# A recurrent attention kernel with a relu-squared MLP: instructions put out in a written order, loads in halves, smaller state transposes

## The chip, the cores and the metric

The kernel runs on one core of a Trainium2 chip. The metric is the time of one execution on the device, in microseconds (us). Each number below is from the hardware profile of one execution, or from repeated timed executions, as the text says.

## The reference

Two stages follow one another. The first walks over 768 positions and keeps a 40 x 40 state for each of 4 batch entries and 8 heads; its output, laid out as 3072 tokens of 320 values, goes through a two-layer MLP with relu squared between the layers.

```python
B, H, S, D = 4, 8, 768, 40
state = np.zeros((B, H, D, D))
for t in range(S):
    y[:, :, t] = np.einsum('bhd,bhde->bhe', r[:, :, t], state)
    Sa = np.einsum('bhde,bhe->bhd', state, a[:, :, t])
    state = state * w[:, :, t][:, :, None, :] - np.einsum('bhd,bhe->bhde', Sa, b[:, :, t]) \
        + np.einsum('bhd,bhe->bhde', v[:, :, t], k[:, :, t])
x = y.transpose(0, 2, 1, 3).reshape(3072, 320)
out = np.maximum(x @ w_in, 0.0) ** 2 @ w_out      # 320 -> 2048 -> 320
```

## The kernel before

**Steps.** The recurrence is computed in blocks of 64 positions, for two batch entries at a time. That gives 12 blocks x 2 pairs = 24 steps, numbered g = 0 to 23; step g continues the state of step g - 2. Each step is a graph of small operations with names. An operation X of step g is called X.g in this text.

**Loads.** LW, LK and LB (line L423) bring w, k and b of the step from device memory through SP's queue, each as two transfers, one for each batch entry. Tiles: Wf, KBf. LA brings a (tile Af), through SP for steps 0 to 3 and through POOL from step 4 on. LV0 and LV1 (L499) bring v, LR (L433) brings r, both through POOL. POOL also brings the MLP weights, wi, wj (tile WIN) and wo (tile WOUT), once. Step 0's LK and LB go through ACT. The buffers of w, k, b and a hold four steps.

**Decay.** LN (ACT, L438) takes the logarithm of w, LO (POOL) its low part, and the matmuls CS and CE (TensorE, the tiles cs and ce) sum it over positions. EXN and EXE (ACT) take exponentials. KBS0 and KBS1 (POOL, L487) scale k and b into KB, AS scales a into A, GLM makes the state's decay.

**Attention.** KB is transposed into KBT: for steps 0 to 5 by TensorE (KT) and a copy, from step 6 on by a DMA transpose that SP issues (KX, L519). AT and RT transpose a and r. EB multiplies KBT with them (L561); EBE masks the product on DVE (L565). XV, X0 and COR form the corrected values x (L576, L584, L598), with ACT copies UA and UB between and MA and MB after (L589, L603). ST (L613, L618) forms the new state, STE (DVE) scales and writes it as STB, SX (L632) transposes it, and SXE (DVE) copies it out as SB. VT (L643), CP, CPE, YC (L657), YS and YE make the output y, and XT and XTE transpose it.

**MLP.** For two halves of the hidden columns: U0 or U1 (L697), then UX and UY (L706) write hp; RL (ACT, L711) applies relu, SQ (DVE, L715) squares it, and D0 to D3 (L724) accumulate fo. OE (ACT) and OST (SP, L735) write the result.

**TensorE's three forms.** Each matmul operation has a mode: M uses the array whole, R splits its rows and C its columns.

**The order.** The kernel is written in one program order; each engine, and each DMA queue, then takes its own instructions strictly in that order, and semaphores make an engine wait for the others. The order comes from the class Plan: it simulates the engines and queues when the kernel is built, with a duration for each operation (the argument dur of add) and costs for each transfer (the argument dma: a number of units and the time of one). Of the operations that an engine could start earliest it takes the one with the lowest place, from the tables PLACE and SHIFT, and adds STAY to the place of one that changes TensorE's mode. Buffers in PSUM come from four rings: S (3 buffers), D, HP and F (one each). Where this simulation leaves TensorE idle ahead of D0.0, the end of the function puts warm-up matmuls (tile warm, L823), of 512 columns each.

Of the kernel before, what the change touches and what calls it, by code (L numbers as in the profile page):

```python
# [32 lines left out]

SHIFT = {}
SHIFT[0] = {
    "zK1": 2018.27, "VT": 2349.81, "AT": 1866.43, "UY0": -3353.72, "KX": -2197.21, "zL0": 1908.62, "zV0": 1900.43,
    "wj2": 1808, "wj1": -1942.98, "EB": 1944.74, "KT": -2891.79, "zF0": 2034.22, "UB": 1935.23, "CS": -2785.17,
    "MA": 2049.64, "U0": 2170.04, "wp0": 2098.6, "KBS0": 1881.72, "RT": 1943.66, "zA1": 2269.37, "RTE": 820.24,
    "EBE": 2195.88, "wo0": 2050.8, "zF2": 2322.28, "SELB": 2324.1, "U1": 1925.05, "TI": 1848.81, "zK2": -2247.96,
    "wi1": -2297.07, "ID": -3595.09, "LV1": 2335.3, "zS1": 2314.64, "ATE": 2366.64, "zL1": 2233.74, "UI": 2813.84,  # L40
    "XT": 2190.97, "zR1": -1897.12, "CE": 2105.63, "LN": -3231.66, "OST": -1905.28, "MB": -1865.15, "X0": 1784.49,
    "CPE": 1714.17, "LV0": 1164.1, "ones": 1737.78, "SEL": 2278.83, "CP": 2605, "UA": -2188.66, "D1": 1958.77,
# [130 lines left out]
class Plan:  # L173
# [3 lines left out]
    DMA_LAG = 2.0  # L177
# [5 lines left out]
    def add(self, name, g, eng, dur, fn, deps=(), mode=None, alloc=None, frees=None, dma=None):  # L183
        o = Op()
# [670 lines left out]
```

## Time and profile before

| quantity | value |
|---|---|
| median of 8 runs | 271.67 us (269.47 to 276.55) |
| the profiled execution: its time | 271.3 us |
| the profiled execution: its span | 269.6 us |
| busy: PE, DVE, ACT, POOL | 246.5, 177.3, 164.2, 164.2 us |
| DMA: moved | 33.75 MB in 111,913 packets |

The span is the part of the execution that the profile covers; 1.7 us of the time lie around it. A busy PE is a bad measure here, since the ends of pipelined matmuls are modelled: the distances from start to start, in the timeline, are of more use. In the views, a line with an engine's name and q (SPq, POOLq) tells of the queue's issuing; PEld is TensorE's weight load.

### The profile page before, as it was taken

How to read it: one execution, taken by the hardware profiler on the slowest of the kernel's cores; microseconds unless marked ns; L12 is line 12 of the kernel's file. 1: busy time of each engine (PE TensorE's matmuls, PEld its weight loads, DVE VectorE, ACT ScalarE, POOL GpSimd, SP SyncE). 2: the span in 40 equal slices, each digit the busy share in tenths (PEclk: the TensorE clock that was granted, in tenths of full speed). 3: DMA queues.
4: the chain of work that ended last, by engine and by line, in shares of the span. 5: the costliest groups of instructions: out<-in, count | busy, mean ns of one | idle time of the engine just before them, and what ended most of it. 6: DMA issues, size and time to landing. Idle time of an engine off the chain costs nothing.

```text
span 269.6 us, 13153 instructions
## 1 busy us (share of the span) xinstructions
PE 246.5 (91%) x5817; PEld 197.6 (73%) x5817; DVE 177.3 (66%) x296; ACT 164.2 (61%) x289; POOL 164.2 (61%) x244
## 2 busy tenths in 40 slices
PE   6869968999989998999999989899999999999980
PEld 2447756697778886878888867788887888888750
DVE  7827756685847865856866856766875866786520
ACT  2355644877657756756866756766775686365440
POOL 2869766994875777576778757678767591400000
PEclk9986999999999999999999999999999999999998
DMA  6999999977999979978979987986989362210010
GB/s 111 155 183 169 189 203 150 154 139 142 124 164 122 162 132 145 150 150 140 165 140 143 120 149 119 156 157 133 127 159 106 83 128 46 62 29 27 12 38 26
DMA packets 111913, 33.75 MB, mean 125 GB/s; under 512 B 101232, under 2 KB 109808, under 8 KB 111856
## 3 DMA queue, kind: packets, MB, share of 16 engines
q1 hardware_dynamic: 100272, 20.79, 51.6%
q0 software_dynamic: 9472, 11.80, 24.3%
q8 instruction: 45, 0.74, 1.2%
q10 hardware_dynamic: 2112, 0.33, 0.7%
q14 instruction: 12, 0.10, 0.1%
HBM read 28.84 MB, written 3.93 MB: 122 GB/s over the span
## 4 chain that ended last, share of the span: by engine, by line
PE 51%; DMA 21%; SPq 15%; ACT 3%; issue 3%; POOL 2%; DVE 2%; POOLq 0%; ACTq 0%; DVEq 0%
SPq L423 15%; PE fo L724 12%; PE hp L706 12%; DMA KBT<-KB 10%; DMA Wf<-in_w_dram 7%; PE hp L697 3%; DMA KBf<-in_b_dram 3%; PE vt L643 2%; PE sx L632 2%; PE rt L532 2%; PE cp L561 2%; ACT RL L711 2%; PE eb L561 2%; PE y L657 2%; DMA KBf<-in_k_dram 1%
## 5 line engine op out<-in xcount | busy, mean ns | idle before, releaser
L487 POOL TENSOR_TENSOR KB<-KBf,EXN 128x320 bf16<-128x320 f32 x45 | 45.4, 1024 | 44.2 <-PE y L657 39.2
L711 ACT ACTIVATE RL<-hp 128x1024 bf16<-128x1024 f32 x46 | 47.1, 1024 | 37.7 <-PE hp L706 37.6
L724 PE MATMUL fo<-WOUT,GT 128*128 128x320 bf16 x384 | 63.1, 299 | 1.1 <-DVE GT L715 1.1
L706 PE MATMUL hp<-XT,WIN 128*128 128x128 bf16 x736 | 52.4, 220 | 0.0
L565 DVE TENSOR_TENSOR EBM<-eb,MASK 128x1024 bf16<-128x1024 f32 x24 | 29.3, 1222 | 29.3 <-PE eb L561 29.2
L706 PEld LDWEIGHTS <-WIN 128*128 128x128 bf16 x768 | 44.1, 98 | 3.9 <-issue 0.3
L715 DVE TENSOR_TENSOR GT<-RL 128x1024 bf16<-128x1024 bf16 x48 | 38.2, 795 | 10.4 <-ACT RL L711 10.4
L724 PEld LDWEIGHTS <-GT 128*128 128x128 bf16 x384 | 33.4, 97 | 12.4 <-DVE GT L715 2.2
L499 POOL DMA_DIRECT2D Vf<-in_v_dram x48 | 33.7, 705 | 0.3 <-issue 0.3
L438 ACT ACTIVATE LNW<-Wf 128x320 f32<-128x320 f32 x24 | 11.2, 468 | 31.5 <-DMA Wf<-in_w_dram 16.2
L565 DVE TENSOR_TENSOR CPM<-cp,MASK 128x1024 bf16<-128x1024 f32 x24 | 29.2, 1216 | 1.4 <-PE cp L561 1.4
L624 DVE TENSOR_TENSOR STB<-st,GLM 128x640 bf16<-128x640 f32 x22 | 18.1, 824 | 15.7 <-PE st L618 13.1
L423 POOL DMA_DIRECT2D Af<-in_a_dram x40 | 27.4, 691 | 0.0
L446 POOL TENSOR_TENSOR LLO<-LNW 128x320 bf16<-128x320 f32 x24 | 17.5, 728 | 9.3 <-ACT LNW L438 9.3
L589 ACT ACTIVATE UZ<-x 64x320 bf16<-64x320 f32 x48 | 20.7, 432 | 3.9 <-PE x L576 2.5
L603 ACT ACTIVATE VM<-x 64x320 bf16<-64x320 f32 x48 | 20.6, 430 | 3.3 <-PE x L598 2.6
L493 POOL TENSOR_TENSOR A<-Af,EXE 128x320 bf16<-128x320 f32 x24 | 20.8, 868 | 1.6 <-DMA Af<-in_a_dram 0.7
L647 DVE COPY VMT<-vt 128x1024 bf16<-128x1024 bf16 x24 | 16.6, 691 | 3.8 <-PE vt L643 2.3
L697 PE MATMUL hp<-XT,WIN 64*128 64x128 bf16 x368 | 18.2, 218 | 0.8 <-ACT RL L711 0.8
L460 ACT ACTIVATE EXN<-cs 128x640 f32<-128x640 f32 x24 | 16.8, 699 | 2.0 <-PE cs L454 1.9
L503 ACT ACTIVATE VM<-Vf 128x640 bf16<-128x640 f32 x24 | 17.6, 733 | 0.5 <-DMA Vf<-in_v_dram 0.2
L729 ACT ACTIVATE OSB<-fo 128x320 f32<-128x320 f32 x24 | 10.4, 434 | 10.1 <-PE fo L724 9.8
(90 smaller groups left out, 459.4 us busy)
## 6 DMA issues: line engine op xcount, KB each, us to landing
Wf<-in_w_dram SPq DMA_DIRECT2D x48, 80.0 KB, 6.0
Vf<-in_v_dram POOLq DMA_DIRECT2D x48, 80.0 KB, 5.4
out_dram<-OSB SPq DMA_DIRECT2D x24, 160.0 KB
KBf<-in_b_dram SPq DMA_DIRECT2D x46, 80.0 KB, 3.2
KBf<-in_k_dram SPq DMA_DIRECT2D x46, 80.0 KB, 6.0
Af<-in_a_dram POOLq DMA_DIRECT2D x40, 80.0 KB, 4.5
RB<-in_r_dram POOLq DMA_DIRECT2D x24, 80.0 KB, 4.4
WOUT<-in_moe_w_out_dram POOLq DMA_DIRECT2D x2, 640.0 KB, 10.7
```

The lines of the kernel that those rows point to most:

```text
L423: q_.dma_start(out=V(dst, step * be, [(40, 8), (1, 40)], 64 * h, 64), in_=tok(src, b0 + be))
L487: (nc.vector if g < 3 and be else nc.gpsimd).tensor_tensor(out=V(kb, 512 * be, [(64, 8), (1, 40)]), in0=V(kbf, 320 * be, [(40, 8), (1, 40) ...
L493: nc.gpsimd.tensor_tensor(out=V(at, 0, [(64, 8), (1, 40)]), in0=V(af, 0, [(40, 8), (1, 40)]), in1=V(exe, 0, [(40, 8), (1, 40)]), op=ALU.mult)
L499: nc.gpsimd.dma_start(out=V(vf, 320 * be, [(40, 8), (1, 40)], 64 - 64 * be, 64), in_=tok(v, b0 + be))
L565: nc.vector.tensor_tensor(out=V(dst, 0, [(64, 16), (1, 64)]), in0=V(psum(key, g), 0, [(64, 16), (1, 64)]), in1=V(MASK, 0, [(0, 16), (1, 64 ...
L589: nc.scalar.activation(out=V(uz, 320 * be, [(1, 320)], 64 * be, 64), in_=V(psum("x", g), 0, [(1, 320)], 64 * be, 64), func=ACTF.Copy, scal ...
L603: nc.scalar.activation(out=V(vm, 512 * be, [(64, 8), (1, 40)], 64 * be, 64), in_=V(psum("x", g), 0, [(40, 8), (1, 40)], 64 * be, 64), func ...
L697: mm(out=V(p, 512 * s + 128 * i, [(1, 128)]), lhsT=wcol(1 + s, blk, 64 * s, 64), rhs=xt[64 * s:64 * s + 64, 128 + 128 * s:256 + 128 * s], ...
L706: mm(out=V(p, 512 * s + 128 * i, [(1, 128)]), lhsT=wcol(x, blk, 0, 128), rhs=xt[:, 128 * x:128 * x + 128], start=False, stop=i == 3 and x > 0)
L711: nc.scalar.activation(out=rl[:], in_=psum(hk, g)[:], func=ACTF.Relu)
L715: nc.vector.tensor_tensor(out=gt[:], in0=rl[:], in1=rl[:], op=ALU.mult)
L724: mm(out=p[:, 0:320], lhsT=gt[:, 512 * s + 128 * i:512 * s + 128 * i + 128], rhs=WOUT[:, DM * blk:DM * blk + DM], start=blk == 0, stop=blk ...
```

## The change

The tables and the choosing simulation are taken out. The program order is now written down as a list, ORDER, of all operations; an entry ~n stands for n warm-up matmuls. Plan only walks through that list, checks that each operation's dependencies have been put out, and hands out the PSUM buffers. The orders of all engines and queues differ from before. The two halves of each load LW, LK, LB and LA become operations of their own, with an a or b at the end of the name, which can stand apart; a half of LK or LB depends only on the KBS of its own half four steps earlier. The names in ORDER show this. The state transposes SX take 104 of STB's 128 rows, since rows 104 to 127 hold no state values, so each of the 8 transposes has a moving operand of 104 columns. The other changed lines alter only numbers that nothing reads any more (the third argument after the engine and dma).

```diff
-PERIOD = 23.56
-PLACE = {
-    "zK1": -384.93, "VT": -379.85, "AT": -379.8, "UY0": -379.8, "KX": -379.8, "zL0": -378.59, "zV0": -366.03,
...
-SWITCH = 0.095
-STAY = 48.55
-WINDOW = {"PE": 0, "ACT": 0, "DVE": 0, "POOL": 0, "SP": 0}
+ORDER = """
+TBL.0 zK1.0 LWa.0 ones.0 UI.0 LWb.0 ID.0 UE.0 LKa.0 LAb.0 MASK.0 zL0.0 SELB.0 LBa.0 LWb.2 zS1.0 zV0.0 LBb.0 zR3.0
+LAa.0 zU1.0 zK0.0 LKb.0 zA0.0 LWa.2 TI.0 LN.0 zR0.0 zR1.0 zR2.0 zF0.0 LO.0 LWb.1 zF2.0 LV1.0 ~8 CS.0 LWa.1 TE.0
+EXN.0 LV0.0 zS0.0 ~1 CE.0 zU0.0 LKb.1 LR.0 zA1.0 zS2.0 EXE.0 KBS0.0 zF1.0 LAb.1 LAa.2 KBS1.0 AS.0 zV1.0 ~6 KT.0
+LAb.2 zL1.0 LN.1 AT.0 wi1.0 ATE.0 LN.2 LR.1 LKa.1 KTE.0 VC.0 LO.2 LAa.1 zV2.0 ~5 EB.0 LO.1 EBE.0 CE.2 LBa.1 wi2.0
+CE.1 SEL.0 LV0.1 EXE.1 XV.0 zF3.0 UB.0 GLM.0 LBb.1 LV1.1 zV3.0 UA.0 zK2.0 ~3 COR.0 LWa.3 wp0.0 LR.2 CS.1 MA.0 wj2.0
+RT.0 MB.0 LWb.3 EXN.1 AS.1 ~1 VT.0 LKb.2 RTE.0 VTE.0 KBS0.1 LWa.4 EXE.2 ~2 AT.1 I2.0 KBS1.1 RT.1 wj1.0 ST.0 ATE.1
+CP.0 GLM.2 KT.1 AS.2 CPE.0 LBb.2 LKa.2 LN.3 LV0.2 KTE.1 VC.1 ~3 CS.2 LBa.2 LV1.2 STE.0 EXN.2 YC.0 LAb.3 wj0.0 RTE.1
+YE.0 EB.1 LO.3 SX.0 LAa.3 EBE.1 LR.3 CE.3 LKa.3 EXE.3 SXE.0 LBa.3 XV.1 KBS0.2 KBS1.2 CS.3 UB.1 AT.2 UA.1 wi0.0 KT.2
+ATE.2 EXN.3 COR.1 LV1.3 KTE.2 RT.2 MA.1 LKb.3 wp1.0 XT.0 MB.1 EB.2 XTE.0 VC.2 LBb.3 AS.3 VT.1 EBE.2 RTE.2 U1.0 LWb.4
+GLM.1 UX1.0 wo0.0 UY1.0 VTE.1 LV0.3 AT.3 RL1.0 LWa.5 ST.1 ATE.3 XV.2 KBS0.3 X0.2 STE.1 LWb.5 CP.1 UB.2 U0.0 KBS1.3
+LBb.4 UY0.0 UA.2 CPE.1 UX0.0 wo1.0 KT.3 RL0.0 LBa.4 SX.1 KTE.3 COR.2 LN.4 SXE.1 YC.1 MA.2 EB.3 LO.4 YE.1 RT.3 MB.2
+XT.1 LAb.4 RTE.3 CE.4 XTE.1 LKa.4 LR.4 SQ0.0 VT.2 EXE.4 LAa.4 ST.2 LKb.4 EBE.3 D0.0 LV0.4 D1.0 VC.3 LWa.6 LV1.4
...
+XTE.3 LWb.9 KBS0.6 EB.5 U0.3 EBE.5 LWb.10 CE.6 LV0.7 VT.4 LBb.8 EXE.6 UY0.3 LV1.7 VC.5 VTE.4 LKb.9 D2.2 AS.6 LN.8
+ST.4 XV.5 LAa.7 STE.4 X0.5 KX.6 CP.4 UB.5 LO.8 UX0.3 CPE.4 UA.5 D3.2 RL0.3 LAa.8 LKa.8 AT.6 COR.5 LAb.8 ATE.6 YC.4
+OE.2 YS.4 RT.7 KBS0.7 MA.5 YE.4 OST.2 U1.3 CS.8 MB.5 SQ0.3 SX.4 LV1.8 EXN.8 XT.4 UY1.3 LR.8 XTE.4 LKa.10 UX1.3 SXE.4
+LAb.7 CE.7 LBb.9 RL1.3 D0.3 KBS1.7 LKb.10 VT.5 LN.9 U0.4 VTE.5 EXE.7 LR.9 EB.6 UY0.4 VC.6 LV0.8 EBE.6 KX.7 UX0.4
+RTE.7 D1.3 LO.9 RL0.4 SQ1.3 ST.5 LBa.8 LAb.9 XV.6 STE.5 X0.6 LWb.11 GLM.6 CP.5 UB.6 AS.7 U1.4 VC.7 UY1.4 SQ0.4 D2.3
+UA.6 CPE.5 D3.3 UX1.4 LWa.10 OE.3 AT.7 RL1.4 LWa.11 YC.5 ATE.7 COR.6 KBS1.8 YS.5 OST.3 RT.8 YE.5 MA.6 CS.9 LBa.10
+LV1.9 SQ1.4 D0.4 MB.6 RTE.8 XT.5 KBS0.8 CE.8 LKa.9 XTE.5 EXN.9 VT.6 LBa.11 D1.4 VC.8 LBa.9 SX.5 EXE.8 EB.7 LKb.11
+LN.10 U0.5 EBE.7 UX0.5 LR.10 UY0.5 LO.10 D2.4 RL0.5 SXE.5 KX.8 AS.8 XV.7 VTE.6 X0.7 ST.6 LAa.9 LWb.14 U1.5 STE.6
+CP.6 LV0.9 D3.4 LBb.11 CPE.6 AT.8 LV1.10 OE.4 UY1.5 UB.7 SX.6 LV0.10 ATE.8 UA.7 UX1.5 SXE.6 GLM.8 LBb.10 CS.10 RL1.5
+LAa.10 SQ0.5 YC.6 OST.4 COR.7 KBS1.9 YS.6 RT.9 MA.7 LWa.12 YE.6 D0.5 EXN.10 KBS0.9 SQ1.5 LKb.12 XT.6 D1.5 MB.7 XTE.6
+RTE.9 EB.8 U0.6 EBE.8 CE.9 KX.9 UX0.6 EXE.9 UY0.6 VC.9 AS.9 VT.7 D2.5 RL0.6 VTE.7 GLM.7 LAb.10 D3.5 SQ0.6 GLM.9 ST.7
+OE.5 XV.8 LN.11 OST.5 STE.7 X0.8 U1.6 UB.8 LO.11 CP.7 LKa.12 UA.8 UX1.6 CPE.7 LKa.11 AT.9 SX.7 LWb.13 UY1.6 ATE.9
+COR.8 RL1.6 YC.7 LWb.12 YS.7 KBS0.10 CS.11 YE.7 LKa.13 D0.6 EXN.11 SQ1.6 KBS1.10 LBb.12 D1.6 MA.8 XT.7 LKb.13 D2.6
+MB.8 LR.11 XTE.7 VC.10 SXE.7 LAb.11 EB.9 LBa.12 U0.7 EBE.9 ST.8 CE.10 KX.10 UY0.7 STE.8 EXE.10 UX0.7 AS.10 VT.8
...
+VTE.11 XV.12 LO.15 RL0.10 LKb.15 RT.13 SQ1.9 X0.12 ST.11 AS.13 LWb.17 VC.13 CP.11 U1.10 CPE.11 LV1.15 UY1.10 RTE.13
+UX1.10 LAa.15 UB.12 AT.13 STE.11 UA.12 D2.9 LBb.15 RL1.10 CS.15 ATE.13 LWb.16 YC.11 COR.12 VC.14 KBS1.14 YS.11 D3.9
+YE.11 MA.12 SX.11 KBS0.14 SQ0.10 OE.9 CE.14 MB.12 OST.9 D0.10 EXE.14 LWa.17 XT.11 EXN.15 D1.10 AS.14 XTE.11 LBa.15
+VT.12 SXE.11 LN.16 LAb.15 SQ1.10 EB.13 LKb.16 U0.11 GLM.13 UX0.11 LAa.16 EBE.13 D2.10 LO.16 UY0.11 KX.14 VTE.12
+RT.14 LAb.16 RL0.11 ST.12 XV.13 LBb.16 LR.15 STE.12 X0.13 CP.12 UB.13 GLM.14 U1.11 CPE.12 UA.13 D3.10 RTE.14 UX1.11
...
+YS.16 COR.17 STE.16 LAa.19 LKa.20 UX1.15 MA.17 UY1.15 LR.20 YE.16 OST.14 MB.17 SX.16 EXN.20 KBS0.19 LWa.22 AT.18
+D0.15 RL1.15 ATE.18 LKb.22 KBS1.19 CE.19 SXE.16 XT.16 D1.15 EXE.19 LV0.20 XTE.16 LN.21 SQ1.15 EB.18 KX.19 LAb.20
+U0.16 ST.17 EBE.18 GLM.18 LO.21 VT.17 LBb.23 UX0.16 LAb.21 VTE.17 LBa.22 UY0.16 D2.15 AS.19 STE.17 RL0.16 XV.18
+X0.18 LAa.20 RT.19 CP.17 RTE.19 LV1.20 U1.16 CPE.17 LKb.21 AT.19 UB.18 D3.15 UA.18 LWb.22 UX1.16 OE.15 SQ0.16 LWb.23
+YC.17 COR.18 KBS0.20 YS.17 ATE.19 OST.15 MA.18 CS.21 YE.17 D0.16 VC.19 KBS1.20 LWa.23 UY1.16 MB.18 XT.17 LV0.21
+EXN.21 SX.17 XTE.17 VT.18 KX.20 LR.21 SXE.17 RL1.16 D1.16 VTE.18 GLM.19 CE.20 SQ1.16 LKa.23 ST.18 EXE.20 LKa.22
...
+D1.21 XTE.22 SQ1.21 CP.23 U0.22 UX0.22 CPE.23 UY0.22 D2.21 RL0.22 D3.21 U1.22 SQ0.22 OE.21 YC.23 YS.23 OST.21 UY1.22
+YE.23 UX1.22 XT.23 D0.22 RL1.22 XTE.23 D1.22 SQ1.22 U0.23 UX0.23 D2.22 D3.22 UY0.23 OE.22 U1.23 RL0.23 OST.22 UY1.23
+UX1.23 SQ0.23 RL1.23 D0.23 SQ1.23 D1.23 D2.23 D3.23 OE.23 OST.23
+"""
...
 class Plan:
...
-    LAG = {"PE": 0.2, "ACT": 0.06, "DVE": 0.06, "POOL": 0.08}
-    DMA_LAG = 2.0
...
+        o.name, o.g, o.eng, o.fn, o.alloc, o.frees = name, g, eng, fn, alloc, frees
+        o.deps = deps
...
+        free = {k: list(range(n)) for k, n in RINGS.items()}
+        self.held, done, order = {}, set(), []
+        for t in ORDER.split():
+            if t[0] == "~":
+                order.append(int(t[1:]))
+                continue
+            name, g = t.split(".")
+            o = self.ops[(name, int(g))]
+            assert all(d in done for d in o.deps if d in self.ops), t
+            if o.alloc and (o.alloc[1], o.g) not in self.held:
+                self.held[(o.alloc[1], o.g)] = (o.alloc[0], free[o.alloc[0]].pop(0))
             if o.frees:
...
+                cls, i = self.held[(o.frees, o.g)]
+                free[cls].append(i)
+            done.add((name, int(g)))
+            order.append(o)
+        assert len(done) == len(self.ops)
+        return order
...
-            def f():
-                for be in range(2):
+            for be in range(2):
+                def f(be=be):
                     h = 1 - be if other else be
                     q_.dma_start(out=V(dst, step * be, [(40, 8), (1, 40)], 64 * h, 64), in_=tok(src, b0 + be))
-            add(name, g, eng, 1.4 if eng == "POOL" else 1.35, f, deps + ([("LN", g)] if eng == "POOL" else []), dma=(64, 0.0065 if eng == "POOL" else 0.014))
-
-        load("LW", wf, 0, w, False, [("LN", g - NL)])
-        load("LK", kbf, 320, k, True, [("KBS0", g - NL), ("KBS1", g - NL)])
-        load("LB", kbf, 320, b, False, [("KBS0", g - NL), ("KBS1", g - NL)])
-        load("LA", af, 0, a, False, [("AS", g - NL)])
+                if eng == "POOL":
+                    add(name + "ab"[be], g, eng, 0.7, f, deps(be) + [("LN", g)], dma=(32, 0.0065, 1.2 + late, 1.2))
+                else:
+                    add(name + "ab"[be], g, eng, 0.68, f, deps(be), dma=(20, 0.0224, 1.15 + late, 0.9))
+
+        load("LW", wf, 0, w, False, lambda be: [("LN", g - NL)])
+        load("LK", kbf, 320, k, True, lambda be: [(f"KBS{be}", g - NL)])
+        load("LB", kbf, 320, b, False, lambda be: [(f"KBS{be}", g - NL)])
+        load("LA", af, 0, a, False, lambda be: [("AS", g - NL)])
 
         def f():
...
-                    nc.tensor.transpose(out=p[:, 128 * i:128 * i + 128], in_=stb[:, 128 * i:128 * i + 128], identity=ID[:])
+                    nc.tensor.transpose(out=p[:, 128 * i:128 * i + 104], in_=stb[0:104, 128 * i:128 * i + 128],
+                                        identity=ID[0:104, 0:104])
...
-    idle, end, each = {}, 1.5, 0.44
-    for o in order:
-        if o.eng == "PE":
-            if o.name == "D0":
-                break
-            idle[o] = max(0, int((o.start - end - 0.3) / each))
-            end, each = o.start + o.dur, 0.22
     warm = ps.tile([128, 512], FP32, name="warm", tag="F0", bufs=1)
     for o in order:
-        for _ in range(idle.get(o, 0)):
-            mm(out=warm[:], lhsT=ones_b[:], rhs=V(ones_b, 0, [(0, 4), (1, 128)]), start=True, stop=True)
-        o.fn()
+        if isinstance(o, int):
+            for _ in range(o):
+                mm(out=warm[:], lhsT=ones_b[:], rhs=V(ones_b, 0, [(0, 4), (1, 128)]), start=True, stop=True)
+        else:
+            o.fn()
 
 
 # ---- launch: one core; inputs and outputs as the reference has them ----
```

## The prediction

> **What bounds the kernel now.** I read the page's slices first, then the waits, then the chain of work that ended last.
>
> ```profile
> PE   6869968999989998999999989899999999999980
> ...
> DMA  6999999977999979978979987986989362210010
> ```
>
> TensorE (PE) and the DMA engines are both nearly full until slice 31 (206 us); then the DMA row drops while PE stays full. So two resources compete to be the bound, and a busy share cannot say which. The waits do:
>
> ```profile
> PE eb L561 <- DMA KBT<-KB: 4.2, 5, 1.3
> ...
> PE st L613 <- ACT VM L603: 1.9, 1, 1.9
> ```
>
> TensorE's main wait for data (total, times, longest, in us) is for the transpose of KB that SP issues at L519. The chain shows why it is late:
>
> ```profile
> 26.71 0.76 SPq L423
> ...
> 29.21 15.18 DMA Wf<-in_w_dram
> ...
> 69.21 0.63 SPq L423
> 69.95 7.37 DMA KBT<-KB
> 77.37 0.41 PE eb L561 x16
> ```
>
> Start and duration in us: SP issues loads (L423) one after another, then the transpose, then TensorE goes on. Two facts follow. The Wf load issued at 29.21 lands only at 44.39, and LN.5 on ScalarE waits for it: until there the start is set by loads. And a transpose stands behind loads that are far from needed. For step 12:
>
> ```profile
> 122.99 2.14 POOL L487 TENSOR_TENSOR KB<-KBf,EXN 128x320 bf16<-128x320 f32 x2 [2.39 <-PE y L657]
> ...
> 131.84 1.29 SPq L519 DMA_TRANSPOSE KBT<-KB  x1
> ```
>
> KB was ready at 125.13, but its transpose was issued at 131.84, 6.7 us later, with 104 loads already through SP's queue.
>
> I then added up TensorE by the starts in the timeline. Undisturbed, each operation has a constant distance to the next: 0.447 us for eight 128-column matmuls, 0.544 for four of 320 columns, 0.253 for the 16 small ones of x or y; a change of tile form adds 0.095. Here is one such step:
>
> ```profile
> 130.65 0.61 PE L706 MATMUL hp<-XT,WIN 128*128 128x128 bf16 x8
> ...
> 131.09 0.61 PE L632 MATMUL sx<-ID,STB 128*128 128x128 bf16 x8
> ...
> 131.64 0.31 PE L454 MATMUL cs<-LNW,TI 64*128 64x320 bf16 x2
> ```
>
> hp to sx takes 0.44, sx to cs (another form) 0.55. In all: 209.2 us of operations, 201 changes of form x 0.095 = 19.1, waits 21.4, warm-up matmuls 6.2. The first real matmul starts at 6.2, so these give the last D3's end at 262.1; 7.5 us of output DMA and end follow, to the span of 269.6. From U1.1 (46.5) to the end the sum without waits is 205.6, so 10.0 us of waits lie there: 5.0 before EB.6, 9, 10, 14 and 19 (all on KBT), 1.3 in the tail, 3.7 in small pieces.
>
> **What the Trainium skill says.** "TensorE: Matmul & The Clock Gate", section "Wait — 56ns, not 53.3ns?": warm matmuls follow each other after N / 2.4 GHz + 2.5 ns, 55.6 ns at N = 128. The trace agrees (0.447 / 8 = 55.9). "TensorEngine Tiling (Array Packing)", "Key Properties": a change of tiling mode drains the array. The trace agrees and prices it at 0.095 us. "Runtime: NRT & Kernel Launch", "Instruction fetch mechanics": instructions arrive in 16 KiB blocks of 256, mostly hidden. The page's queue q8 agrees: 45 packets, 0.74 MB, and 11,634 PE instructions / 256 = 45. The steady stretch 120 to 155 us holds no stop over 0.06 us, so most are hidden here; one stop of 0.89 us (169.6, amid the A transposes) has no clear data cause and may be one. "DMA: Bandwidth & Descriptors", "Issuing engines are not separate DMA queues": SP's and POOL's transfers share the same 16 engines. From 70 to 206 us the DMA share is 0.92 in this trace, in accord.
>
> **The change, part by part.**
> *State transposes.* 8 matmuls x 22 steps stream 104 columns, not 128. By the skill's formula (an estimate) 45.8 instead of 55.8 ns: 22 x 8 x 10 ns = 1.8 us off TensorE. Bounds: 0 if the issue limits, 1.8; I take 1.8.
> *The order on TensorE.* I counted the new ORDER's PE entries: the same 598 operations, but 219 changes of form, 18 more: +1.7 us. Sum without waits: 228.3 before, 228.2 after. 29 warm-up matmuls instead of 33 lie in the start's idle time: 0. So TensorE's work does not shrink; only waits can.
> *Turnarounds.* I compared the TensorE work that the new order puts between a producer and its consumer with the shortest distance in the trace (EB to XV 1.73, COR to VT 1.61, CP to YC 1.84, and so on), and likewise for the PSUM buffers' reuse (1.73 for D, 1.75 for HP). After step 1 only five are short (YS.6, CP.14, XV.15, VT.16 to their consumers, U1.1's buffer), by 0.08, 0.20, 0.16, 0.02 and 0.11. The in-order ACT, DVE and POOL queues, filled with the page's mean durations, never hold over 1.5 us of backlog after step 6. So no new wait is built in: 0.6 us at most.
> *SP's queue.* Loads are now entered one batch half at a time and later. Loads ahead of each transpose, before and after: KX.6 62, 60; KX.8 76, 73; KX.10 90, 86; KX.12 104, 93; KX.15 122, 110; KX.19 148, 137. From KX.7 (81.47) to KX.19 (200.33) SP passed 80 loads, 12 outputs and 12 transposes in 118.9 us, 1.14 us each, though an unhindered issue takes 0.64: the queue ran at the pace of the transfers. Eleven loads fewer are 11 x 1.14 = 12.5 us, more than the 6.7 that KX.12 was late: it will wait for KB, not for the queue. From KX.8 to KX.20 70 loads remain, 5.8 per step, with output and transpose 7.8 x 1.14 = 8.9 us per step, below TensorE's 9.54: DMA stops setting the pace. A load behind a KX waits until KB is ready; that is late next. POOL's queue keeps its instructions (an LA pair is the same two issues of 0.69); moved among them, they cost 0, since POOL idles 39.2 us ahead of KB for y's matmuls.
> *The start.* LW.1 and LW.2 move ahead in SP's queue (issues 4 to 8 instead of 9, 10, 15 and 16), so the 2.0 us stop before ST.0 and the half clock after it (17.9 to 24.7 us) should go. But Wf of step 5 stays issues 31 and 32, and the weights on POOL's queue keep their place, so I leave 44.4. In the new ACT order LN.5, then RL0.1, then TensorE's U1.1 follow: 44.5 + 0.47 + 1.0 + 0.3 = 46.3. What was gained earlier waits there. Bounds: 44.3 (fewer early bytes) and 52 (loads reordered against the weights).
> *Sum.* From U1.1 on the new order holds 204.8 us (form changes and the 104 columns in it): 46.3 + 204.8 = 251.1. Waits: tail 1.3 (the same last entries); EB.6: KX.6 has two loads fewer ahead, so 69.95 - 2 x 1.27 (the mean issue from 29.21 on) = 67.4, plus 5.2 to 7.4 to land, 72.6 to 74.8, where TensorE arrives at 72.7: 1.0; other late loads 1.4; small pieces 1.7 of the 3.7. Together 5.4: 256.5. With 7.5 of tail, span 264.0; the profiled execution took 271.3 for a span of 269.6, so + 1.7 = 265.7. The profiled execution is 0.4 below the median of 8 runs (271.67), so 265.8 is what I give. A measurement of this kernel can tell about 0.5% (1.4 us) from no change.
>
> **The rivals.**
> *A, forecast:* SP's backlog goes, KBT waits shrink: 265.8, its own range 259.5 to 269.5. Chance 0.75.
> *B, DMA keeps the pace:* the same bytes must move, and 0.92 of the engines was already used while TensorE ran 0.4 us per step behind. If the start (Wf of step 5 at 50 instead of 44.4) or the transfers' pace gives nothing, the 6 us are lost: 271.5. For it: the loads were backpressured from 13 us on. Against it: 8.9 us per step above. Chance 0.11.
> *C, late loads:* slower. LWb.16 stands only 3.9 us of TensorE work ahead of LN.16, LWa.10 4.6, LWb.6 5.0, LWb.22 5.5, against a median landing of 6.0 us. LN stands in ScalarE's in-order queue, and RL, UA/UB and MA/MB behind it feed TensorE directly. The forecast leaves 6 us for about 20 steps: from 0.3 us lost per step on this decides. At 0.9 per step for 18 steps (the mean of the shortfalls 2.1, 1.4, 1.0, 0.5 less a little cover): 251.1 + 1.3 + 3.1 + 16 = 271.5, + 9.2 = 280.7; at half of it 272.7. Against it: SP is not tied to TensorE and runs ahead when its queue is short. Chance 0.14.
> *D, the fetch:* that the model now knows instruction fetches is worth the 0.9 us stop at most; inside A.
>
> **How the numbers follow.** 265.8 is A. The low end 259.5: U1.1 at 44.4 and only the tail's waits, 44.4 + 204.8 + 1.3 + 9.2. The high end 273 takes in B and half of C. Faster by over 0.5% 0.75 (A), same 0.11 (B), slower 0.14 (C).
>
> **What would show it.** Right: KX.12 issued within 1 us of KB's end; no KBT wait after EB.8; TensorE's sum without waits near 228 with sx-to-next 0.08 shorter; DMA busy to about slice 32 at a lower share; U1.1 near 46. Wrong: LNW waits on Wf after 60 us (C), U1.1 after 50 or KBT waits as before (B), or sx at 0.447 still.

## The result, and the profile after

| | before | after |
|---|---|---|
| median, measured side by side, us | 272.27 | 274.19 |
| ratio after / before | | 1.0128, 95% interval 1.0087 to 1.0168 |
| profiled execution: time, span, us | 271.3, 269.6 | 272.68, 270.9 |

The change made the kernel slower by 1.3%; 265.8 was forecast. Ratios here and below compare the undisturbed executions of a kernel with those of before measured beside it, so they can differ from the quotient of the medians; e1 and e16 gave too few for a ratio. The slices of the page after:

```profile
PE   5986899979999998999999979999998999999980
PEclk9999799997999999999999999999999999999996
DMA  6999999697999996996497997698899767610110
```

The DMA row has dips in the middle (slices 18 and 19) that before had not, and stays at 6 to 7 up to slice 34, where before's falls to 3 at 31 and to 2 at 33. The clock row has a 7 in slice 9 (61 to 68 us), just after TensorE had stood still. What stood still shows in TensorE's waits of after (engine, line, releaser: total us, times, longest):

```profile
PE kt L355 <- POOL KB L331: 3.2, 2, 2.0
...
PE cp L405 <- issue: 1.1, 1, 1.1
...
PE eb L405 <- DMA KBT<-KB: 1.0, 2, 0.7
PE hp L551 <- issue: 0.9, 1, 0.9
PE y L510 <- issue: 0.9, 1, 0.9
...
PE y L502 <- issue: 0.5, 1, 0.5
```

The wait that the forecast was about, eb on KBT, fell from 4.2 us to 1.0. In its place came KT.5, waiting for KB (2.0 of the 3.2 us), and four lines "issue", where nothing that the profile shows was waited for. First the KX.12 that the prediction followed, in the timeline of after (GpSimd, then SP):

```profile
126.07 1.27 POOL L331 TENSOR_TENSOR KB<-KBf,EXN 128x320 bf16<-128x320 f32 x1
...
127.36 1.25 SPq L363 DMA_TRANSPOSE KBT<-KB  x1
```

KB is done at 127.34 and the transpose is issued 0.02 us later (6.7 before): the queue no longer holds it. Then the chain of after around KT.5:

```profile
48.81 0.03 SPq L580
...
50.30 8.13 DMA KBf<-in_b_dram
...
59.47 0.87 POOL KB L331
...
60.39 0.62 PE kt L355 x8
```

SP has issued the first output store (L580) by 48.8 and LBb.5 at 50.30, three entries later; that half load takes 8.13 us to land, KB of step 5 waits for it, and KT.5 starts 2.1 us late. From 61.1 to 64.5 the clock that TensorE is granted is 0.50, which costs some 1.7 us more (half of 3.4, an estimate). Last, two of the "issue" stops in TensorE's timeline of after:

```profile
102.89 0.20 PE L510 MATMUL y<-SB,ART 128*64 128x80 bf16 x1
103.98 0.30 PE L510 MATMUL y<-SB,ART 128*64 128x80 bf16 x7 [0.89 <-issue]
...
205.82 0.96 PE L551 MATMUL hp<-XT,WIN 128*128 128x128 bf16 x14
207.70 0.27 PE L551 MATMUL hp<-XT,WIN 128*128 128x128 bf16 x2 [0.92 <-issue]
```

A stop amid eight or sixteen matmuls on the same operands is hardly a wait for data. I counted TensorE's instructions (two for a matmul, and its semaphore instructions): these stops stand after instruction 192 or 193 of each 256, counted from the first one in the trace. I take this place for the end of a block of 256 instructions (why it isn't at 256 isn't shown). Each stop ends 2.4 to 3.0 us after one of the 45 transfers of q8, the instruction queue, has started. Over all 20 traces of this study, 56 of the 64 pauses of over 0.45 us inside one operation (from 30 us on) stand at this place. I call them block stops: 5.3 us in eight in after, 4.8 of them after U1.1; 2.1 us in two in before (at 35.4 and 170.0), 0.9 after U1.1. In before q8's transfers start 1.18 us (mean) after TensorE has passed the end of a block, in after 1.75.

The ends without a stop tell as much. With q8's transfers and the block ends of the 20 traces paired in order (the first end has none), TensorE passes 855 ends from 30 us on, and not one of them sooner than 2.2 us after the transfer has started. 57 times it got to an end within 2.0 us of that start, and each time it stood for over 0.2 us; of the 750 times that it came 2.4 us after the start or later, it stood for over 0.4 us in 9. So it is the fetch that is waited for, and two times decide whether a stop comes: how late the fetch starts, and how fast TensorE runs through the block.

The views of the stretch 176 to 215 us (length; busy PE, PEld, DVE, ACT, POOL; clock; DMA share; GB/s), before and then after:

```profile
176.00:215.00 39.00, 38.43 (x1001) 32.05 (x997) 27.46 (x39) 26.12 (x47) 27.47 (x40) 1.00 0.80 130
```

```profile
176.00:215.00 39.00, 37.58 (x968) 31.11 (x958) 26.30 (x40) 24.91 (x47) 24.81 (x37) 1.00 1.00 138
```

Loads that before has behind it are still under way in after: the engines' share is 1.00, not 0.80. Two of the stops lie here (206.6 and 213.4).

### The profile page after: what moved, and what is told of

It reads as the page before. It is cut to its first block, busy times and chain, and to the rows that moved or that the text cites. A ratio compares the mean times of both kernels' runs of the same rounds, so it can differ in the third digit from the quotient of the medians.

```text
span 270.9 us, 13116 instructions
## 1 busy us (share of the span) xinstructions
PE 247.7 (91%) x5813; PEld 196.0 (72%) x5813; DVE 178.8 (66%) x296; ACT 162.8 (60%) x289; POOL 162.1 (60%) x244
## 2 busy tenths in 40 slices
DMA packets 111913, 33.75 MB, mean 125 GB/s; under 512 B 101232, under 2 KB 109808, under 8 KB 111856
## 4 chain that ended last, share of the span: by engine, by line
PE 60%; DMA 18%; SPq 5%; ACT 5%; POOL 3%; DVE 3%; issue 3%; POOLq 0%; ACTq 0%
PE fo L569 13%; PE hp L551 12%; DMA Wf<-in_w_dram 8%; DMA KBf<-in_b_dram 5%; PE hp L542 4%; DMA KBT<-KB 3%; SPq L264 3%; PE vt L488 3%; PE cs L298 2%; PE y L502 2%; PE x L442 2%; PE sx L476 2%; PE eb L405 2%; PE cp L405 2%; ACT RL L556 2%
## 5 line engine op out<-in xcount | busy, mean ns | idle before, releaser
L569 PE MATMUL fo<-WOUT,GT 128*128 128x320 bf16 x384 | 65.6, 301 | 0.6 <-DVE GT L560 0.5
L331 POOL TENSOR_TENSOR KB<-KBf,EXN 128x320 bf16<-128x320 f32 x45 | 39.9, 898 | 37.5 <-PE y L502 26.2
L551 PE MATMUL hp<-XT,WIN 128*128 128x128 bf16 x736 | 53.3, 222 | 0.9 <-issue 0.9
L551 PEld LDWEIGHTS <-WIN 128*128 128x128 bf16 x768 | 45.4, 99 | 4.9 <-issue 1.2
L560 DVE TENSOR_TENSOR GT<-RL 128x1024 bf16<-128x1024 bf16 x48 | 37.0, 771 | 9.2 <-ACT RL L556 9.1
L337 POOL TENSOR_TENSOR A<-Af,EXE 128x320 bf16<-128x320 f32 x24 | 21.4, 894 | 21.5 <-ACT EXE L320 11.7
L515 DVE TENSOR_TENSOR YB<-y,EXE 128x320 bf16<-128x320 f32 x24 | 11.8, 490 | 13.6 <-PE y L510 13.3
```

Source lines behind the costliest of these rows:

```text
L331: (nc.vector if g < 3 and be else nc.gpsimd).tensor_tensor(out=V(kb, 512 * be, [(64, 8), (1, 40)]), in0=V(kbf, 320 * be, [(40, 8), (1, 40) ...
L337: nc.gpsimd.tensor_tensor(out=V(at, 0, [(64, 8), (1, 40)]), in0=V(af, 0, [(40, 8), (1, 40)]), in1=V(exe, 0, [(40, 8), (1, 40)]), op=ALU.mult)
L551: mm(out=V(p, 512 * s + 128 * i, [(1, 128)]), lhsT=wcol(x, blk, 0, 128), rhs=xt[:, 128 * x:128 * x + 128], start=False, stop=i == 3 and x > 0)
L560: nc.vector.tensor_tensor(out=gt[:], in0=rl[:], in1=rl[:], op=ALU.mult)
L569: mm(out=p[:, 0:320], lhsT=gt[:, 512 * s + 128 * i:512 * s + 128 * i + 128], rhs=WOUT[:, DM * blk:DM * blk + DM], start=blk == 0, stop=blk ...
```

## The experiments

Two theories were set against each other. **Transfers:** up to about step 12 the transfers set TensorE's time whatever the order, and a late one is only replaced by another. **Fetch:** the time is lost at instruction blocks, whose fetch waits among data transfers. A third, **stores**, came out of the runs. EB.6, EB.12 and so on are the start of that operation in the profiled execution; before has EB.6 at 77.4, EB.12 at 136.4, EB.20 at 213.0 and the last D3 at 261.6; after has 75.8, 135.2, 214.1 and 262.9. Such starts compare only within one order of TensorE: ahead of EB.12 the old order has D2.9, D3.9, U0.10 and VT.11 as well, some 1.8 us of work by the prediction's distances (an estimate), so that after, with 135.2, is not ahead of before there.

| run | order of TensorE, ACT, DVE, POOL | order of SP | EB.6 | EB.12 | block stops, us | median, us | ratio to before |
|---|---|---|---|---|---|---|---|
| before | before | before | 77.4 | 136.4 | 2.1 | 272.27 | |
| after | after | after | 75.8 | 135.2 | 5.3 | 274.19 | 1.0128 |
| e2 | before | after | 83.9 | 141.2 | 4.1 | 272.41 | 1.003 |
| e3 | after | before | 85.7 | 145.2 | 5.7 | 282.58 | 1.040 |
| e5 | before | before, KX earlier | 77.9 | 139.0 | 6.1 | 274.68 | 1.0075 |
| e6 | after | after, LB.5 earlier | 72.0 | 136.0 | 7.3 | 275.01 | 1.0008 |
| e7 | before | before, then after | 75.6 | 136.9 | 4.6 | 271.65 | 1.0017 |
| e9 | after, fewer v loads | after | 72.5 | 130.6 | 3.1 | 267.5 | 0.9893 |
| e10 | before, fewer v loads | before | 73.7 | 133.3 | 2.9 | 266.17 | 0.989 |
| e12 | as e7, 18 stores late | as e7 | 74.0 | 132.1 | 5.3 | 317.07 | 1.167 |
| e13 | as e7, 6 stores later | as e7 | 74.1 | 130.8 | 6.2 | 283.78 | 1.041 |
| e14 | after, 6 stores later | after | 75.8 | 133.2 | 6.4 | 290.2 | 1.054 |

### Parts of the change

**e1**, the order of before, with the 104-column transposes alone:

```diff
-  nc.tensor.transpose(out=p[:, 128 * i:128 * i + 128], in_=stb[:, 128 * i:128 * i + 128], identity=ID[:])
+  nc.tensor.transpose(out=p[:, 128 * i:128 * i + 104], in_=stb[0:104, 128 * i:128 * i + 128],
+                      identity=ID[0:104, 0:104])
```

> The order of before, written out as a list, with only the state transposes cut to 104 columns. Three theories of why the changed kernel came out slower: F, TensorE now stops at the ends of its 256-instruction blocks for the next block (5.0 us of such stops after U1.1 in its trace against 0.9 before); L, loads come late, above all LB of step 5, for which KT.5 waited 2.1 us and then ran 1.4 us longer at half clock; S, the 18 further changes of form, 1.7 us, eat what the small transposes give. All three expect the transposes to be worth 22 x 0.079 = 1.7 us where TensorE is the bound: ratio to before 0.994. If they are hidden behind the KBT waits of the old order: 1.000, with the KBT waits longer by about 1.5 us.

Measured: 275.95 against 271.72, no ratio; its six executions lie between 265.97 and 277.27. In its profile U1.1 came at 48.8 and EB.19 waited 3.3 us for KBT. Inconclusive: a gain of 1.7 us doesn't show beside executions that differ by more.

**e11**, the reverse of it in the kernel after:

```diff
-  ... in_=stb[0:104, 128 * i:128 * i + 128], identity=ID[0:104, 0:104])
+  ... in_=stb[:, 128 * i:128 * i + 128], identity=ID[:])
```

> The kernel after, with the state transposes at 128 columns again and nothing else changed. If TensorE's own work sets the end: 22 x 0.079 = 1.7 us longer, ratio 1.006. If waits on transfers set it, the saved time is only a longer wait elsewhere: ratio 1.000 within 0.3%. In the trace sx to next 0.447 instead of 0.368 either way.

Measured: 275.32, ratio to before 1.0283 [1.0106, 1.0459]. Beside after's own 1.0128 the intervals overlap, so the size isn't settled. Its timeline shows the largest stop of the new order:

```profile
79.21 0.22 PE L442 MATMUL x<-UZ,EBM 128*64 128x40 bf16 x3
83.19 0.52 PE L442 MATMUL x<-UZ,EBM 128*64 128x40 bf16 x13 [3.76 <-issue]
```

Three of sixteen equal matmuls, then nothing for 3.8 us: again after instruction 192 of a block, and the fetch had started only at 80.08, 5.3 us after the end of the block before.

**e2**, the order of before on all engines but SP, with 104 columns:

```diff
-... LBa.7 LBb.7 LWa.10 LWb.10 LKa.8 LKb.8 LBa.8 LBb.8 KX.6 OST.2 LWa.11 LWb.11 ...
+... LBa.7 LWa.9 LKa.7 LKb.8 LWb.9 LWb.10 LBb.8 LKb.9 KX.6 LKa.8 OST.2 LKa.10 ...
```

> The order of before on TensorE, ACT, DVE and POOL, with SP's queue in the order of the changed kernel, and 104-column transposes. F: TensorE's order is the old one, so its block ends cost 1 us as before, and the KBT waits (5.0 us) go: 272.3 - 1.7 - 4 = 266.5, ratio 0.979. L: the later loads are what costs, so LB.5 is late here too: KT.5 waits 2 us and the clock halves, and other loads are late: 270 to 274, ratio 0.99 to 1.005. S: 1.7 us of form changes are spared: ratio 0.985.

**e3**, the reverse: the kernel after with SP's entries of before:

```diff
-... LBa.7 LWa.9 LKa.7 LKb.8 LWb.9 LWb.10 LBb.8 LKb.9 KX.6 LKa.8 OST.2 LKa.10 ...
+... LBa.7 LBb.7 LWa.10 LWb.10 LKa.8 LKb.8 LBa.8 LBb.8 KX.6 OST.2 LWa.11 LWb.11 ...
```

> The changed kernel with SP's queue in the order of before. F: the stops at block ends stay near 5 us, and KBT waits come back: 274 to 277, ratio to before 1.007 to 1.017. L: KT.5's wait and the half clock after it (3.6 us) go, KBT waits of 2 to 5 us come back: 270 to 274, ratio 0.99 to 1.005. S: as the changed kernel, 1.013.

Measured: e2 1.003 [0.9998, 1.0062], e3 1.0399 [1.0337, 1.0462]. In e2 the KBT waits are gone and twelve steps from EB.6 to EB.18 take 114.2 us (118.7 in before), but four waits of 1.7 to 3.0 us ahead of it (KT.1, amid YS.2, after XT.2, KT.5) bring EB.6 6.5 us late: gained and given back. The one amid YS.2 is a block stop, and so is another of 1.5 us at 77.3. In e3 the waits on KBT return (8.3 us in five), and its U1.1 comes at 54.7. So SP's order does decide the KBT waits, as the prediction had it, and nothing is won.

### Instruction blocks

**e4**, the kernel after with 128 TensorE instructions more ahead of the first real one:

```diff
-  for _ in range(o):
-      mm(out=warm[:], ... V(ones_b, 0, [(0, 4), (1, 128)]) ...)
+  for _ in range(72 if first else o):          # first group: 72 of 57 columns for 8 of 512
+      mm(out=warm[:, 0:c_], ...)
```

> The changed kernel, but its first warm-up group has 72 matmuls of 57 columns instead of 8 of 512 (the same 3.4 us of work at half clock): 128 TensorE instructions more ahead of everything, so each block of 256 ends half a block earlier in the work. F: the stops of over 0.2 us move from YS.7, CP.13, UY0.17 and CE.21 to other places 64 matmuls earlier, and their sum changes by 1 to 4 us, most likely down, since the four were the worst: 270 to 274. L and S: no change within 0.5%: 274.2, ratio to before 1.008 to 1.017, and KT.5 waits 2 us as before.

Measured: 276.37, ratio 1.0105 [1.0021, 1.0189]. The stops at 102.9, 159.8, 206.6 and 213.4 are gone, and others stand at 35.9, 43.5, 54.1, 83.6, 151.4, 162.6, 199.7 and 211.6 (0.4 to 1.9 us; 8.6 us in all), again after instruction 192 or 193 of their blocks. So the stops belong to block ends, not to the operations at which they stood.

**e8**, the same in before (144 instructions more):

```diff
-  for _ in range(o):
+  for _ in range(81 if first else o):          # first group: 81 of 57 columns
```

> The kernel before in its own order and with its 128-column transposes, its first warm-up group made of 81 matmuls of 57 columns instead of 9 of 512: 144 TensorE instructions more ahead. F: TensorE's old order has no places where 256 instructions run through within 3.4 us of the block before, so the shift brings at most one or two stops of about 1 us: ratio 0.997 to 1.008. If the old order was only lucky in where its blocks end, it gets the 5 us of the changed kernel: 1.015 to 1.02.

Measured: 276.07, ratio 1.0181 [1.0059, 1.0302]. The two stops of before (35.4 and 170.0) are gone, and others stand at 37.4, 42.6 (2.1 us), 62.0 and 126.0: 4.5 us. But TensorE stands 5.9 us after CS.1 as well (ST.0 waits for VM; U1.1 at 51.5), so the ratio is not that of the fetch alone. What holds is that the old order pays these stops too, by where its blocks end.

**e9** and **e10**, the kernels after and before without the v loads from step 4 on (3.3 of 33.75 MB; those steps multiply old v):

```diff
   def f(be=be):
+      if g >= 4:
+          return
       nc.gpsimd.dma_start(out=V(vf, 320 * be, ...
```

> The kernel after, with the two v loads of every step from step 4 on left out (those steps multiply stale v; the order is otherwise the same): 40 DMA issues and 3.3 of 30.3 MB fewer. If the pace of the transfers sets TensorE's time up to about step 12, the late LB.5 (2.1 us before KT.5, then half clock) and the KBT wait before EB.8 (1.1) go: EB.12 at 129 to 132 instead of 135.3, and the ratio is 0.975 to 0.985. If the order itself or instruction fetch is what costs, EB.12 stays within 1 us of 135, the ratio is 0.99 to 1.01. On the block stops (5.0 us in the kernel after): if they are the fetch queued among data transfers, the delay from one block to the next fetch falls from 1.75 us and the stops to below 2 us; if the dense small matmuls alone use up a block faster than it can be fetched, 4 us and more stay.

> The kernel before, with the two v loads of every step from step 4 on left out (those steps multiply stale v). If the transfers' pace bounds it, as theory one says, the five KBT waits go, six steps from EB.6 to EB.18 take 114.5 us instead of 118.7 for twelve steps, and the ratio is 0.975 to 0.985. If SP's order alone held the transposes (each SP issue at its own 0.64 us), the queue still carries every SP load, the waits stay, and the ratio is 0.99 to 1.0.

Measured: 0.9893 [0.9852, 0.9934] and 0.989 [0.972, 1.006]. EB.12 comes at 130.6 in e9 (135.2 in after) and at 133.3 in e10 (136.4 in before), so with less to move TensorE gets there sooner in both orders. In e9 the fetches start 1.30 us after a block's end (1.75 in after) and the block stops after U1.1 fall from 4.8 to 1.8 us. With lighter traffic the two orders tie: what after loses goes with its traffic. One rival stands: the 40 loads left out also spare GpSimd 40 issues of 0.7 us, and GpSimd makes KB, so part of the gain may be GpSimd's; no run tells the two apart.

### The order of the loads

**e5**, before with each KX from 6 to 19 moved ahead of four loads (and 104 columns):

```diff
-... LBa.7 LBb.7 LWa.10 LWb.10 LKa.8 LKb.8 LBa.8 LBb.8 KX.6 OST.2 ...
+... LBa.7 LBb.7 LWa.10 LWb.10 KX.6 LKa.8 LKb.8 LBa.8 LBb.8 OST.2 ...
```

> The order of before with the 104-column transposes, and each transpose KX of steps 6 to 19 moved four load issues forward in SP's queue. If the KBT waits are a matter of the queue (the prediction's step), KX comes 4 x 1.14 = 4.6 us earlier, still behind its KB, and the 5.0 us of KBT waits fall under 1: 272 - 4 - 1.7 = 266, ratio to before 0.975 to 0.985. If the transfers' pace itself is the bound (loads late instead), the waits move to Wf or KBf: 0.993 to 1.005.

Measured: 1.0075 [0.9996, 1.0153]. The KBT waits are gone, and instead AT.6 waits 1.3 us for A, and block stops of 2.2 (112.5) and 1.5 us (181.6) stand where before had none: 6.1 us of them in all. It looks as if a wait for a transpose had given the fetch its time.

**e6**, after with LB.5 ahead of LWa.7, so that KT.5 gets its KB:

```diff
-LWa.6 LWb.6 LWa.7 LKb.5 LWb.7 LWa.8 LKa.5 OST.0 LKb.6 LKa.6 LBb.5 LBa.5 LBb.6
+LWa.6 LWb.6 LBb.5 LBa.5 LWa.7 LKb.5 LWb.7 LWa.8 LKa.5 OST.0 LKb.6 LKa.6 LBb.6
```

> The changed kernel with the two halves of LB.5 moved in front of LWa.7 in SP's queue, eight issues earlier. L: KT.5's wait (2.1 us) and the half clock after it (1.4 us) go: 274.2 - 3.5 = 270.7, ratio to before 0.99 to 1.00. F: the stops at block ends stay (about 5 us), so that the gain is partly kept: 0.998 to 1.006. If step 5's load only trades places with another late load: 1.01 as the changed kernel.

Measured: 1.0008 [0.9939, 1.0077]. TensorE's first wait in it:

```profile
PE eb L403 <- DMA KBT<-KB: 5.5, 3, 4.1
```

KT.5 starts at 56.8 and EB.6 3.8 us earlier than in after; then EB.8 waits 4.1 us, and EB.12 comes at 136.0, no earlier than in after. One late transfer was replaced by another.

**e7**, the order of before on all engines but SP, SP's of before up to step 7 and of after from there:

```diff
-... LBa.7 LBb.7 LWa.10 LWb.10 LKa.8 LKb.8 LBa.8 LBb.8 KX.6 OST.2 LWa.11 LWb.11 ...
+... LBa.7 LBb.7 LKb.8 LWb.10 LBb.8 LKb.9 KX.6 LKa.8 OST.2 LKa.10 LBb.9 LKb.10 KX.7 ...
```

> The order of before with the 104-column transposes; SP's queue in the order of before up to LB.7 (56 loads), then what is left in the order of the changed kernel. In e2 the whole of the changed SP order made the start 6.6 us later (EB.6 at 84.0 for 77.4), then EB.6 to EB.18 took 114.3 us without a KBT wait, where the kernel before took 118.7. If start and steady part are separate, EB.6 comes at 75 to 78 and D3 ends near 257: 266, ratio 0.975 to 0.985. If the late start belongs to the late loads in general (loads of steps 6 to 8 come later here too): 0.99 to 1.003. F: no block end stops of note, since TensorE's order is the old one.

Measured: 1.0017 [0.9964, 1.007], a tie, though no KBT wait over 0.5 us is left. EB.12 is at 136.9, and its pauses of 1.2 (90.4), 1.6 (101.3), 0.7 and 0.8 us are block stops again: 4.6 us.

### The output stores

**e12**, e7 with the stores of steps 0 to 17 behind SP's last load:

```diff
-  OSB = ring("OSB", 2, 320, FP32)
+  OSB = ring("OSB", 20, 320, FP32)
...
-  ... LKb.23 ... (OST.0 to OST.17 each in its step)
+  ... LKb.23 OST.0 OST.1 OST.2 ... OST.17 ...
```

> The kernel of e7 (TensorE, ScalarE, VectorE and GpSimd in the order of before, SP's order of before up to step 7 and of after from there, 104-column state transposes), with the output stores of steps 0 to 17 (18 x 160 KB) held in a larger ring until SP has issued its last load. Nothing is left out: 2.9 of some 30 MB move from the time before 205 us to the time after it, where the DMA share is 0.22, and SP passes 18 issues fewer ahead of the transposes. If the transfers' pace (or SP's queue) up to 200 us is what costs, as e9 and e10 say, this gains about as much as leaving out the v loads did: ratio 0.985 to 0.992. If what counts is the number of small packets (an output store has 128 of 1280 bytes, a v load 512 of 160 bytes), it gains little: ratio 0.998 to 1.004, as e7. If the held stores then run into the tail: above 1.005.

Measured: 1.1669 [1.1585, 1.1754]. The chain says why:

```profile
230.87 3.23 SPq L578
...
234.14 3.22 SPq L578
...
264.01 13.78 DMA KBT<-KB
...
277.84 0.61 PE eb L403 x15
```

Each store (L578) took 3.2 us where nothing else moved, and KX.20 stood behind them, which I hadn't foreseen. From 225 to 260 us the DMA view of this kernel has q1 (packets, MB, share of 16 engines) at

```profile
q1 hardware_dynamic: 1371, 1.73, 13.3%
```

49 GB/s, and a busy share that is little more than that of two of the 16 engines. (The destination of a store has an outermost dimension of two, one for each batch entry; whether that is why isn't shown.) But up to there it was the fastest kernel with all its loads so far: EB.12 at 132.1, EB.20 at 206.3 (213.0 in before).

**e13** and **e14**, e7 and after with the stores of steps 0 to 5 alone moved, each behind that of the step 8 later:

```diff
-  OSB = ring("OSB", 2, 320, FP32)
+  OSB = ring("OSB", 10, 320, FP32)
...
-  ... OST.8 LBa.14 ... OST.9 LWa.17 ...
+  ... OST.8 OST.0 LBa.14 ... OST.9 OST.1 LWa.17 ...
```

> The mixed order of e7 with only the output stores of steps 0 to 5 held (ring of 10 instead of 2): SP issues each behind the store of the step 8 later, so that all transposes keep few issues ahead and the end is not touched. If stores and SP's queue up to step 12 are what costs there: EB.12 at 132 to 133.5 as in e12 (132.3) instead of 136.9 in e7, EB.20 at 207 to 209, ratio 0.98 to 0.988. If e12 was early by chance of the execution: EB.12 at 135 to 137, ratio 0.997 to 1.005.

> The kernel after with the same six output stores moved later and nothing else. If late transfers up to step 12 and the block stops are two separate costs: the KBT wait before EB.8 (1.1) and part of the wait before KT.5 go (stores start at about 72 us, so KT.5 at 58 is not touched), EB.12 at 133 to 134 instead of 135.3, and 3 us and more of block stops stay: ratio 1.000 to 1.008. If all its loss is traffic, it comes to the time of e13: 0.98 to 0.99. If the moved stores in the second half make the fetches later still, it stays at 1.013 or above.

Measured: 1.0407 [1.0334, 1.048] and 1.0537 [1.0444, 1.0629]. EB.12 comes at 130.8 (136.9 in e7) and 133.2 (135.2 in after): the first half did what was expected. In the second, e13's TensorE waits begin with

```profile
PE eb L404 <- DMA KBT<-KB: 9.7, 7, 2.6
```

Behind two stores side by side the loads and transposes come late. So in these traces the stores belong to what sets the pace, in both orders; moved ones spaced evenly weren't tried.

**e15**, **e16** and **e17**: e7, after, and before (with 104 columns), with the stores issued by ScalarE:

```diff
-  nc.sync.dma_start(out=dst, in_=osb[:])
-  add("OST", g, "SP", 0.6, ...
+  nc.scalar.dma_start(out=dst, in_=osb[:])
+  add("OST", g, "ACT", 0.6, ...
```

> The mixed order of e7 with all output stores issued by ScalarE, behind the copy that feeds them, on ScalarE's own DMA queue. If a store blocks what stands behind it in SP's queue for up to 3.2 us: EB.12 at 131 to 132.5 (136.9 in e7), EB.20 at 206 to 208, span 260 to 264, ratio 0.972 to 0.985. If only bytes or issues count, the same bytes move at the same time: EB.12 at 135 to 137, ratio 0.995 to 1.005. ScalarE pays 0.6 us per step; where that is late for TensorE, up to 0.01 more.

> The kernel after with all output stores on ScalarE's queue, nothing else changed. Stores as the cause of the late transfers: EB.12 at 131 to 133 instead of 135.3, no KBT wait; the block stops are another cost and stay at 2 to 5 us: ratio 0.985 to 0.997, slower than e15 by the stops. If the late transfers are only bytes: EB.12 at 135, ratio 1.01.

> The kernel before with 104-column state transposes and all output stores on ScalarE's queue, its order unchanged. Here 104 loads still stand ahead of the transpose of step 12. If the stores are what slowed SP's queue, its KBT waits go (4.2 us and what follows them) although the order is unchanged: ratio 0.975 to 0.988. If the order of loads and transposes is the cause, as the prediction had it, the waits stay: ratio 0.993 to 1.0.

Measured: 1.0221 [1.0134, 1.0308]; 281.1 against 272.35, no ratio; 1.0143 [1.0063, 1.0223], where the median of e17, 271.92, lies under the 272.35 of before beside it, so that e17 isn't shown to be slower. All three lose 3 to 6 us around 55 us, at the first store. The chain of e17:

```profile
54.15 3.75 DMA KBf<-in_b_dram
...
57.98 1.13 ACTq L578
...
59.22 0.55 ACT VM L345
```

The store waits for a load that SP issued at 54.15: in the trace's operands the transfers of SP and ScalarE raise eight semaphores in turn, and each first waits for the one before on its own. ScalarE stood 6.5 us, with VM behind it. After that e17, in before's own order of loads and transposes, has no wait over 0.5 us up to the tail, and 0.2 us of block stops: from KT.5 to the last D3 193.9 us (201.3 in before). But its KT.5 starts at 68.4, 8.2 us later than in before (60.2), which gave SP's queue that much time, so this doesn't show that the stores had held the transposes up. e16, in the order of after, keeps 4.7 us of block stops, e15 4.4.

**e18**, before (104 columns) with the stores on GpSimd's queue:

```diff
-  nc.sync.dma_start(out=dst, in_=osb[:])
-  add("OST", g, "SP", 0.6, ...
+  nc.gpsimd.dma_start(out=dst, in_=osb[:])
+  add("OST", g, "POOL", 0.6, ...
```

> The kernel before in its own order of loads and transposes, with 104-column state transposes and all output stores issued by GpSimd (each placed behind the GpSimd instruction that runs when its data are ready). If the stores in SP's queue held up the loads and transposes: no KBT wait over 0.5 us, KT.5 at 58 to 61, then 194 us as in e17 to the last D3: span 260 to 264, ratio 0.965 to 0.98, faster than before and after. If the order of loads and transposes, as the prediction had it, is what costs: KBT waits as before (4.2), ratio 0.993 to 1.0. If GpSimd's 0.6 us per store, or its queue's share of the engines, makes KB or the loads of a, v and r late: above 1.0, with waits on KB, A or VM.

Measured: 1.0512 [1.0339, 1.0685], another miss. The chain of e18, and the DMA row of its stretch from 78 to 100 us in 40 slices:

```profile
93.81 0.36 PE y L500 x16
94.17 4.44 issue
98.62 0.34 PE y L508 x8
```

```profile
DMA  9999925119699999999999958899999999799999
```

The old TensorE order, too, stands 4.4 us at a block's end, where all DMA engines are busy and the fetch starts at 95.47, 5.9 us after TensorE had come to the end of the block before (89.56); two more block stops of 2.0 and 0.9 us lie ahead of it. Until then KX.6 to KX.9 were issued 3.1 to 6.2 us after their KB, though no store stood in SP's queue: the stores alone had not held them up. From EB.8 (104.3) on, 7.8 us later than in before, only AT.23 waits over 0.5 us ahead of the tail: 160.8 us to the last D3, 165.0 in before. Of the versions that do all the work, none is shown to beat before.

## Why the prediction was wrong

| term, us | predicted | measured in after |
|---|---|---|
| U1.1 | 46.3 | 45.0 |
| operations and form changes from U1.1 | 204.8 | the same counts and distances |
| block stops after U1.1 | at most 0.9 | 4.8 |
| late loads, KT.5 above all | 1.4 | 2.1, and 1.7 of half clock |
| KBT waits | 1.0 | 1.0 (EB.8 and EB.14) |
| tail | 1.3 | 0.7 |
| small pieces | 1.7 | 3.4, what is left |
| last D3's end | 256.5 | 263.5 |

*TensorE's work: right.* SX to the next takes 0.368 us, not 0.447, 1.7 us in 22 steps; 18 changes of form more take it back. The start came 1.3 us earlier than forecast. (Two slips of arithmetic, too small to matter: 265.7 and 0.4 make 266.1, and the low end comes to 259.7.)

*The fetch, the step that failed.* The forecast lowered the waits after U1.1 to 5.4 us, and put the fetch among them at nothing of its own: "worth the 0.9 us stop at most", inside A. That bounded the loss by what before showed. I looked for what the change could save and not for what it could add: its loads come later, the engines are at 1.00 instead of 0.80 from 176 to 215 us, and fetches wait among them. The stops came to 4.8 us after U1.1, 3.9 more than in before and more than the 3.2 won at KBT. The stop of 1.1 us amid KT.3 in before (35.4, "issue") I hadn't recognised as one. The stretch of 120 to 155 us without a stop, taken as a sign that fetches are hidden, held for that order and that execution only. The Trainium skill, "Runtime: NRT & Kernel Launch", "Instruction fetch mechanics", calls the cost of crossing a block mostly hidden; here a block costs nothing at most of its 45 ends, and up to 4.4 us where data fill the engines (e18).

*Late loads, the second term that was mis-sized: right mechanism, wrong place.* The prediction looked at LW and left 1.4 us; 3.8 were lost by LB.5, behind a store (8.13 us to land). LNW did wait for Wf, the sign of C, at steps 10, 16 and 22 (87.6, 146.0 and 208.1; 1.1 to 2.9 us), three of the four that C names. It cost little: TensorE stood for at most 0.3 us at a time behind them.

*SP's queue: right for the transposes, too much concluded.* That KX.12 would wait for KB and not for the queue was right, to 0.02 us. From KX.6 to KX.19 a transpose was issued 5.8 us (mean) after its KB in before and 2.1 us in after, and the KBT waits came to the forecast 1.0. SP itself issued at the same pace: from KX.7 to KX.19 it was busy for 112.2 of 118.9 us with 104 entries in before, and for 101.6 of 119.8 us with 97 in after, 1.08 and 1.05 us each. And e2 goes from EB.6 to EB.18 at 9.5 us per step with all the traffic, TensorE's pace as forecast. But "DMA stops setting the pace" left out the start and the fetches. Every order with the full traffic on SP's queue reaches EB.12 at 135 us or later; only leaving out v loads or moving early stores brought it under 134. This much of rival B, with 0.11, came true.

*Signs that didn't tell.* What the prediction named as signs of being right came: KX.12 within 1 us of KB, no KBT wait over 0.3 us after EB.8, sx to next 0.08 shorter, U1.1 near 46. They stood where a gain was looked for, and none where the loss came.

*What stays open.* How much of the stops belongs to the new order. In the seven traces with its TensorE order and the full traffic they come to 6.6 us on average (4.7 to 8.6), in the eleven of the old order to 4.4 (0.2 to 7.8); these kernels differ in more than that order, and each trace is one execution. That the fetch is waited for rests on q8's start times at 855 block ends, and on e4, e8 and e9; why a fetch starts late where the engines are full was not tested, and a kernel without fetches wasn't tried. The small pieces of 3.4 us were not taken apart.

## What to carry to other kernels

Before counting on a shorter queue, ask what comes late instead: fewer issues in front of an urgent transfer moved that one here, and LB.5 came late in its place. Give early stores, which nobody waits for, a price in the queue that they stand in. And where the DMA engines are full, instruction fetch is one more transfer: price it from the fullest stretch that the new order makes, not from the profile of the old one.

## What the runs showed that I had not expected

- TensorE stops amid equal matmuls after instruction 192 or 193 of a block of 256, for up to 4.4 us. In 84 stops of over 0.4 us at this place the matmuls go on 2.8 us (median; 2.4 to 3.2 in eight of ten) after the fetch has started, though its packet takes 0.9 to 1.7 us.
- An output store of 160 KB in 128 packets takes 3.2 us alone, on an eighth of the engines' time (49 GB/s in e12), while loads of 80 KB in 512 packets reach 140 GB/s and more together with the rest of the traffic.
- SP's and ScalarE's transfers take their semaphores in one common turn of eight; a store on ScalarE waited 6.5 us for a load that SP issued late.
